# Attention and a gated FFN on one core: weight conversions moved some rounds later in the first stage, and the early FFN products dealt out anew

## The chip, the cores and the metric

One core of a Trainium2 chip runs the whole kernel in one launch. The metric is the device time of one execution in microseconds (us); the time before is the median of three runs, 660.65 us. TensorE is called PE here, VectorE DVE, ScalarE ACT, GpSimd POOL; SP is the queue that issues the DMAs.

## The reference

```python
# q, k, v: (4, 12, 448, 64), causal attention; its output as x: (1792, 768) float32
scores = where(mask, -1e9, q @ k.T / 8)
attn = exp(scores - max); attn = attn / (sum(attn) + 1e-9)
x = (attn @ v) reshaped to (B*S, H*D)
# FFN, d_ff = 1536
xn = x / sqrt(mean(x*x) + 1e-6) * rms_g
g = xn @ w_gate
out = ((g * sigmoid(g)) * (xn @ w_val)) @ w_out
```

## The kernel before, in words

The tokens are worked through in three groups. The first stage, some 50 us, is the attention of the first group, and everything in the change lies in it. It has 12 units p0 to p11 (a pair of heads, 256 queries). A unit goes through five steps: the scores on PE (L209), mask, maximum and subtraction on DVE (`softmax`, L225, four instructions), the exponentials with their sums on ACT (L228, four), the reciprocal sums `rs` on DVE (L239) and the scaling by them ("norms", L233, four instructions, on POOL save for p0 in part and p11, which is scaled on ACT, L231), then two sets of transposes on PE (L280: into bank `t` for the first head, into bank `x` for the second), their copies `pt` to SBUF (the first by ACT L286 or DVE L284, the second by DVE L284), and the products with v on PE (L309). Two units give one chunk c of x (0 to 5; p11 completes chunk 5). A chunk stands in PSUM, bank `a` or `y`, and `first_chunk` makes three things from it: `xh` (ACT, L396), the rounded value; `xl` (DVE, L397), its remainder; and `sq` (ACT, L346), its squares, which are added up in `acc` (POOL L107, for the last chunk DVE L348). `sq` has one buffer.

The column sums of `acc` (PE, L405) start the chain of the root mean square: a root on ACT (L414), reciprocal and diagonal on DVE (L417, L419), and a spreading product on PE (L423).

Beside the attention the first weight tiles s = 0, 1, 2, ... of the FFN are prepared. They come as 64-bit values (`load_w`, L456, three buffers) and are turned into float32 by `convert_ops`: `w_c` on ACT (L479), a shift on DVE (L480), a merge on DVE (L482), and a store (L484). `split_w` then makes the pair `w_h` (ACT, L492) and `w_l` (DVE, L494). A product "s1c4" is weight tile 1 with chunk 4 of x: three matmuls (L538, L539, L540) that need `w_h`, `w_l`, `xh` and `xl`. Fifteen of them (tiles 0 to 2, chunks 0 to 4) are laid into the first stage as early products, and the rest follow tile by tile.

The order is written out by hand. The stage is a list of steps, six to a round: in a round PE gets the scores of p+3, the products of p and the transposes of p+1. After each step a clock `now` ticks. `post(n, f)` puts f n ticks later, and the tables LOAD, CONVERT, SPLIT, SHIFT and MERGE give the tick of each weight tile's load and four preparing steps; READY_W and READY_X give the tick from which an early product may stand. Each engine works through its instructions in the order so made, and SP its DMAs; the times come from what they wait for. From tick 94 on the list ends and tile after tile is multiplied.

Of the kernel before, what the change touches and what calls it, by code (L numbers as in the profile page):

```python
# [14 lines left out]
ALU = mybir.AluOpType  # L15
# [8 lines left out]
NP = H // 2  # L24
# [13 lines left out]
for i in range(2 * 2 * NP, len(UNITS), NP):  # L38
    UNITS[i + 3: i + 6] = UNITS[i + 4: i + 6] + UNITS[i + 3: i + 4]
LAST = {(g, c): max(i for i, u in enumerate(UNITS) if u[0] == g and u[2] == c)  # L40
        for g in range(NG) for c in range(NP)}
# [3 lines left out]


T = dict(c0=0, c2=4, c3=4, c26=5, c36=5, c5=6, c56=7, exp=1, exp0=3, gt=1, hh=1, hl=4, ws=5, ld2=7,
         ld=4, ld1=11, lv=2, norm0=7, norm=6, norm1=2, r0=2, sq=1, acc=7, acc4=7, dg=0, spread=3, r1=5, so=3, wl=2, wl0=8, wl2=9, wl4=1, xl=2, xl0=9)
LOAD = (1, 15, 27, 37, 48, 60, 72, 84)
CONVERT = (16, 28, 38, 50, 64, 85, 88)  # L50
SPLIT = (34, 46, 58, 70)
SHIFT, MERGE = (24, 44, 54, 68, 78), (30, 46, 56, 70, 80)

READY_W, READY_X = (45, 57, 68), (40, 52, 64, 76, 87)
WR = 4
WARM = [6, 0, 0, 0]
EXTRA = 4
# [9 lines left out]
def attention_ffn(ctx: ExitStack, tc: tile.TileContext, qk0, qk1, qk2, v, v2, w, g, out, out2):  # L67
# [7 lines left out]
    nc = tc.nc  # L75
# [22 lines left out]
    def bank(tag, bufs=1):  # L98


        return ps.tile([P, W], F32, tag=tag, name=tag + "_ps", bufs=bufs)

    def f32(ap):
        return ap.bitcast(F32)

    def pool_op(out_, a, op, b):
        nc.gpsimd.tensor_tensor(out_, a, b, op=op)  # L107
# [28 lines left out]
    def post(delay, fn):  # L136
        if delay <= 0:
            fn()
        else:
            later.setdefault(now[0] + delay, []).append(fn)  # L140
# [7 lines left out]
    xr, xh, xl, acc, xq = {}, {}, {}, {}, {}  # L148
# [141 lines left out]
    def steps_a(p):  # L290


        if not 0 <= p < len(UNITS):
            return []
        g_, kind, c, k, _, base = UNITS[p]
        pr = hs[p]
        kb, nq = KB[kind], QUERIES[kind]

        def products():
            if g_ == 0 and base == 0:  # L300
                av[c] = bank("y").rearrange("p (s c) -> p s c", s=2) if c % 2 else av_ps
            at_ = av[c] if g_ == 0 else av_ps
            for h in range(1 + (kind == 2)):
                at = 0
                for j in range(NKB[kind]):
                    q0, n = ((0, 2 * P), (P, P))[j] if kind == 0 else (D * h, (P, D)[kind - 1])
                    a0 = at + (D * h if kind == 2 else 0)
                    for e in (0, 1):
                        nc.tensor.matmul(  # L309
                            at_[e * D: (e + 1) * D, p % 2, q0: q0 + n], raw_v[p][:kb, h, j, e, :],  # L310
                            pr["pt", e][:kb, a0: a0 + n], start=(j == 0), stop=(j == NKB[kind] - 1))
                    at += n if kind == 0 else P

        def copy():
            if p == ENDS[0] - 2:
                post(3, lambda: nc.scalar.activation(warm_up, eps, AF.Sqrt))
            if g_ == 0:
                if p == LAST[g_, c]:
                    x = av[c].rearrange("p s c -> p (s c)")
                    post(2, lambda: first_chunk(c, x))  # L320
                return
            if g_ == 2 and base == 0:
                if c < 3:
                    xq[c] = w64_p.tile([P, 2, XT], F32, tag="w64", name="xq")
                xr[g_, c] = xq[c % 3][:, c // 3]
            elif base == 0:
                xr[g_, c] = xr_p.tile([P, W], F32, tag="xr", name="xr")
            x = xr[g_, c][:, base: base + nq]
            if p == LAST[g_, c]:
                for j in range(1 + (g_ == 2)):  # L330
                    post(2 + j * (c < NP - 1), lambda j=j: square(g_, c, j))
            (nc.scalar.copy if g_ == 1 else nc.vector.tensor_copy)(x, av_ps[:, p % 2, :nq])

        return [products, copy]
# [4 lines left out]
    def first_chunk(c, x):  # L339

        last = c == NP - 1
        sq = rm_p.tile([P, W], F32, tag="sq", name="sq") if c else \
            rm_p.tile([P, W], F32, tag="acc", name="acc", bufs=2)

        def squares():
            nc.scalar.activation(sq, x, AF.Square)  # L346
            if last:
                nc.vector.tensor_tensor(acc[0, 0], acc[0, 0], sq, op=ALU.add)  # L348
                post(T["r0"], lambda: rms_first(column_sums(acc[0, 0])))
            elif c == 0:  # L350
                acc[0, 0] = sq
            else:
                post(T["acc"] if c < NP - 2 else T["acc4"], lambda: pool_op(acc[0, 0], acc[0, 0], ALU.add, sq))

        if last:
            squares()
        x_split(0, c, x)
        if not last:
            post(T["sq"], squares)

    sq2 = []

    def square(b, c, j):

        lo, hi = (HX * j, HX * (j + 1)) if b == 2 else (0, W)
        if c and j:
            if not sq2:
                sq2.append(rm_p.tile([P, W], F32, tag="rms", name="sq2", bufs=2))
            sq = sq2[0]
        else:  # L370
            sq = rm_p.tile([P, W], F32, tag="sq", name="sq") if c else \
                rm_p.tile([P, W], F32, tag="acc", name="acc", bufs=2)
        sq = sq[:, : hi - lo]
        nc.scalar.activation(sq, xr[b, c][:, lo: hi], AF.Square)  # L374
        if c == 0:
            acc[b, j] = sq
        else:
            post(3 if c < NP - 1 else 0, lambda: pool_op(acc[b, j], acc[b, j], ALU.add, sq))
        if b == 2:
            return  # L380
        if c == NP - 1:
            post(T["r1"], lambda: rms(b, [acc[b, 0]]))
        waiting.append((b, c))

    def split_x():
        if not waiting:
            return
        b, c = waiting.pop(0)
        x_split(b, c, xr[b, c])

    def x_split(b, c, x):

        gc = g_sb[:, c: c + 1]
        h = xx_p.tile([P, W], F32R, tag=f"xh{c}", name="xh")
        l = xx_p.tile([P, W], F32R, tag=f"xl{c}", name="xl")
        nc.scalar.mul(h, x, gc)  # L396
        post(T["xl0" if b == 0 and c < NP - 1 else "xl"], lambda: nc.vector.scalar_tensor_tensor(  # L397
            out=l, in0=x, scalar=gc, in1=f32(h), op0=ALU.mult, op1=ALU.subtract))
        xh[b, c], xl[b, c] = h, l

    def column_sums(sq):

        ps = bank("t")[:, : W // P]
        for i in range(W // P):
            nc.tensor.matmul(ps[:, i: i + 1], sq[:, P * i: P * (i + 1)], ones[:, :1],  # L405
                             start=True, stop=True)
        return ps
# [56 lines left out]
    def convert_ops(s):  # L464
# [6 lines left out]
        hf_ = raw_w.bitcast(F32)[:, :, 1]  # L471
        at2, at3, at5 = [T[n] for n in ("c26 c36 c56" if s < len(CONVERT) else "c2 c3 c5").split()]
        if s < len(MERGE):
            at2, at3, at5 = SHIFT[s] - CONVERT[s], MERGE[s] - CONVERT[s], MERGE[s] - CONVERT[s] + 8

# [11 lines left out]
    def split_w(s):  # L487
        if s < 2 * NU:
            t = wt[s]
            h = ws_p.tile([P, DM], F32R, tag="wh", name="w_h")  # L490
            l = ws_p.tile([P, DM], F32R, tag="wl", name="w_l")
            nc.scalar.copy(h, t)  # L492
            if s < NU + 2 * NF or s % 2:
                post(T[("wl0", "wl0", "wl2", "wl2", "wl4")[s] if s < 5 else "wl"], lambda: nc.vector.tensor_tensor(l, t, f32(h), op=ALU.subtract))  # L494
            else:
                post(T["wl"], lambda: pool_op(l, t, ALU.subtract, f32(h)))
            wt[s] = tuple(a.rearrange("p (k m) -> p k m", m=P) for a in (h, l))
            u = s - NU
            if 0 <= u < 2 * NF:
                pair[u % 2] = t  # L500
                if u % 2:
                    post(T["ws"], lambda v=u // 2, t0=pair[0], t1=t: quad_sums(v, t0, t1))
# [404 lines left out]
    with tc.manual_schedule():  # L907
# [25 lines left out]

        for fs, at_ in ((load_w, LOAD), (lambda n: convert(n), CONVERT), (split_w, SPLIT)):
            for n, t_ in enumerate(at_):
                at_tick(t_, lambda fs=fs, n=n: fs(n))
# [13 lines left out]
        def convert(s):  # L950
            for d, op in convert_ops(s):
                post(d, op)
# [12 lines left out]
        for s in range(2 * NU):  # L965
# [5 lines left out]
            if s % NU == 0:  # L971
                at, goal = done, ends[w_ + 1]
            if len(LOAD) <= s + 7 < NU:
                post(T["ld"], lambda s=s: load_w(s + 7))
# [6 lines left out]
            for k0 in (0, 2, 4):  # L981
# [7 lines left out]
                if w_ == 0 and i >= 73 and (i % 2 or i > 100):  # L989
                    split_x()  # L990
                if k0 == (0 if s < 3 else 4) and s + 3 >= len(SPLIT):
                    split_w(s + 3)
                if k0 == 4 and s + 5 >= len(CONVERT):
                    convert(s + 5)
# [127 lines left out]
```

## Time and profile before

| | |
|---|---|
| median of 3 runs | 660.65 us (660.17 to 661.35) |
| profiled execution | 660.94 us, of it 659.1 us in the span |
| PE busy | 650.7 us (99%) |
| DVE, ACT, POOL busy | 494.1 (75%), 388.7 (59%), 302.5 us (46%) |
| PE busy, 0 to 21.7 us | 19.94 us |
| PE busy, 21.7 to 30 us | 6.53 us of 8.30 |

Times below count from the start of the span. A matmul's listed time overlaps the next one's; what a sequence costs PE is the distance from start to start. On the other engines too a listed time ends some 0.1 us after the next instruction has started, so the distance of starts is the price there as well.

### The profile page before, as it was taken

How to read it: one execution, taken by the hardware profiler on the slowest of the kernel's cores; microseconds unless marked ns; L12 is line 12 of the kernel's file. 1: busy time of each engine (PE TensorE's matmuls, PEld its weight loads, DVE VectorE, ACT ScalarE, POOL GpSimd, SP SyncE). 2: the span in 40 equal slices, each digit the busy share in tenths (PEclk: the TensorE clock that was granted, in tenths of full speed). 3: DMA queues.
4: the chain of work that ended last, by engine and by line, in shares of the span. 5: the costliest groups of instructions: out<-in, count | busy, mean ns of one | idle time of the engine just before them, and what ended most of it. 6: DMA issues, size and time to landing. Idle time of an engine off the chain costs nothing.

```text
span 659.1 us, 12064 instructions
## 1 busy us (share of the span) xinstructions
PE 650.7 (99%) x4154; PEld 552.0 (84%) x4154; DVE 494.1 (75%) x1024; ACT 388.7 (59%) x852; POOL 302.5 (46%) x300
## 2 busy tenths in 40 slices
PE   9899999999999999999999999999999999999997
PEld 6567777777877787877787878888999999999997
DVE  6988997788886676767677663595776866889992
ACT  6996767766875567666666655435433434355540
POOL 4760403345543066886768788643424342402220
PEclk9999999999999999999999999999999999999999
DMA  8885997888896448585848655235666366473541
GB/s 284 287 257 204 293 282 237 291 292 236 260 322 222 137 146 277 188 297 191 255 156 252 206 183 196 88 118 184 240 218 230 123 225 218 152 221 96 156 144 61
DMA packets 71501, 138.82 MB, mean 211 GB/s; under 512 B 7760, under 2 KB 39376, under 8 KB 71440
## 3 DMA queue, kind: packets, MB, share of 16 engines
q1 hardware_dynamic: 71440, 138.05, 64.4%
q8 instruction: 33, 0.54, 0.3%
q14 instruction: 28, 0.23, 0.1%
HBM read 104.21 MB, written 33.82 MB: 209 GB/s over the span
## 4 chain that ended last, share of the span: by engine, by line
PE 90%; ACT 4%; DVE 2%; POOL 1%; issue 1%; DMA 1%; SPq 0%; DVEq 0%; POOLq 0%; ACTq 0%
PE m_ps L538 15%; PE m_ps L540 14%; PE m_ps L539 14%; PE s_ps L689 9%; PE m_ps L689 9%; PE a_ps L309 6%; PE t_ps L280 5%; PE y_ps L689 5%; PE x_ps L689 4%; PE s_ps L209 2%; ACT sp L228 2%; PE s_ps L217 1%; POOL sp L233 1%; PE x_ps L209 1%; PE x_ps L217 1%
## 5 line engine op out<-in xcount | busy, mean ns | idle before, releaser
L233 POOL TENSOR_SCALAR sp<-sp,rs 128x128 f32<-128x128 f32 (+3 forms) x162 | 126.2, 796 | 146.3 <-DVE rs L239 128.8
L538 PE MATMUL m_ps<-xh,w_h 128*128 128x512 f32 x276 | 117.1, 424 | 0.0
L540 PE MATMUL m_ps<-xh,w_l 128*128 128x512 f32 x276 | 108.3, 392 | 0.0
L539 PE MATMUL m_ps<-xl,w_h 128*128 128x512 f32 x276 | 108.2, 392 | 0.0
L228 ACT ACTIVATE sp<-sp,nm 128x128 f32<-128x128 f32 (+3 forms) x168 | 87.2, 522 | 12.1 <-DVE nm L225 12.1
L107 POOL TENSOR_TENSOR a_l<-w_q,a_h 128x768 fp32r<-128x768 f32 x24 | 47.9, 1996 | 79.6 <-ACT a_h L580 78.2
L286 ACT COPY pt<-t_ps 128x384 f32<-128x384 f32 (+1 forms) x69 | 34.3, 497 | 65.5 <-PE t_ps L280 65.2
L540 PEld LDWEIGHTS m_ps<-xh,w_l 128*128 128x128 f32 x276 | 51.9, 188 | 11.9
L538 PEld LDWEIGHTS m_ps<-xh,w_h 128*128 128x128 f32 x276 | 51.9, 188 | 11.4 <-issue 3.3
L539 PEld LDWEIGHTS m_ps<-xl,w_h 128*128 128x128 f32 x276 | 52.1, 189 | 8.0 <-issue 0.2
L538 PE MATMUL m_ps<-hh,w_h 128*128 128x512 f32 x144 | 58.1, 404 | 0.0
L280 PE MATMUL t_ps<-ident,sp 128*128 128x128 f32 (+1 forms) x348 | 56.9, 275 | 1.2 <-POOL sp L233 0.6
L280 PEld LDWEIGHTS t_ps<-ident,sp 128*128 128x128 f32 (+1 forms) x348 | 42.7, 137 | 18.3 <-POOL sp L233 4.2
L107 POOL TENSOR_TENSOR w_r<-w_r 128x384 f32<-128x384 f32 x48 | 51.6, 1085 | 12.2 <-DVE w_l L494 11.3
L540 PE MATMUL m_ps<-hh,w_l 128*128 128x512 f32 x144 | 56.2, 390 | 0.0
L539 PE MATMUL m_ps<-hl,w_h 128*128 128x512 f32 x144 | 56.2, 390 | 0.0
L225 DVE CUSTOM_DVE_ANT_0 sp<-s_ps,mask 128x128 f32<-128x128 f32 (+3 forms) x108 | 41.0, 428 | 19.7 <-PE s_ps L217 9.6
L309 PEld LDWEIGHTS a_ps<-pt,v_r 128*64 128x64 f32 (+1 forms) x816 | 36.5, 137 | 16.2 <-issue 6.9
L309 PE MATMUL a_ps<-pt,v_r 112*64 112x64 f32 (+2 forms) x816 | 46.1, 262 | 1.8 <-ACT sp L228 1.6
L580 ACT CAST a_h<-w_q 128x768 fp32r<-128x768 f32 (+1 forms) x48 | 35.0, 753 | 13.3 <-DMA w_q<-wz 5.6
L479 ACT ACTIVATE w_c<-w 128x768 f32<-128x768 f32 x36 | 33.0, 917 | 7.1 <-DMA w<-in_w 7.1
L107 POOL TENSOR_TENSOR acc<-acc,sq 128x384 f32<-128x384 f32 (+1 forms) x19 | 23.4, 1236 | 29.6 <-ACT sq L374 27.8
(212 smaller groups left out, 1661.1 us busy)
## 6 DMA issues: line engine op xcount, KB each, us to landing
w<-in_w SPq DMA_DIRECT2D x36, 768.0 KB, 5.2
w<-w_c SPq DMA_DIRECT2D x36, 384.0 KB, 5.7
w_r<-w SPq DMA_DIRECT2D x36, 384.0 KB, 5.0
qk_r<-in_qk SPq DMA_DIRECT2D x48, 256.0 KB, 5.1
qk_r<-in_qk SPq DMA_DIRECT2D x12, 512.0 KB, 4.1
v_r<-in_v SPq DMA_DIRECT2D x12, 448.0 KB, 4.8
v_r<-in_v SPq DMA_DIRECT2D x24, 192.0 KB, 4.2
wy<-w_r SPq DMA_DIRECT2D x24, 192.0 KB, 5.0
```

The costliest lines, as they stand in the source:

```text
L107: nc.gpsimd.tensor_tensor(out_, a, b, op=op)
L225: nc.vector.tensor_tensor_reduce(out=sp, in0=ps, in1=mk, scale=nsc, scalar=3.0e38, op0=ALU.add, op1=ALU.min, accum_out=nm)
L228: post(T["exp" if p >= ENDS[0] else "exp0"], lambda: nc.scalar.activation(sp, sp, AF.Exp, bias=nm, scale=-1.0, accum_out=sm))
L233: pr["norms"].append(lambda: (nc.gpsimd if p or not e else nc.vector).tensor_scalar(sp, sp, rs, 1.0, op0=ALU.mult, op1=ALU.mult))
L280: nc.tensor.transpose(ps[:kb, at: at + P], pr["sp"][e][:, o + kb * j: o + kb * (j + 1)], ident)
L286: nc.scalar.copy(pt[:kb, :at], ps[:kb, :at])
L309: nc.tensor.matmul(at_[e * D: (e + 1) * D, p % 2, q0: q0 + n], raw_v[p][:kb, h, j, e, :], pr["pt", e][:kb, a0: a0 + n], start=(j == 0), st ...
L538: nc.tensor.matmul(ps, wh[:, k, :], mh, start=(first and k == ks[0]), stop=False)
L539: nc.tensor.matmul(ps, wh[:, k, :], ml, start=False, stop=False)
L540: nc.tensor.matmul(ps, wl[:, k, :], mh, start=False, stop=(last and k == 5))
L580: nc.scalar.copy(h, src)
L689: nc.tensor.matmul(ps, a[x], b[y], start=first and n == 0, stop=last and n == 2, skip_group_check=True)
```

## The change

Three tables and some delays change; no instruction is added or taken away. Tile 1 is shifted and merged later (ticks 44 and 46 become 55 and 60); tiles 2, 3 and 4 are converted at 52, 64 and 88 in place of 38, 50 and 64; the splits of tiles 1, 2 and 3 stand at 61, 81 and 91 in place of 46, 58 and 70; the loads of tiles 4 to 7 move from 48, 60, 72, 84 to 61, 72, 87, 95. Chunks 1 to 3 of x are taken from PSUM six ticks later, with `xl` three ticks behind `xh` in place of nine and the squares six ticks behind in place of one. Tile 1 is ready for products from tick 69 (57 before), tile 2 from 87 (68).

```diff
-         ld=4, ld1=11, lv=2, norm0=7, norm=6, norm1=2, r0=2, sq=1, acc=7, acc4=7, dg=0, spread=3, r1=5, so=3, wl=2, wl0=8, wl2=9, wl4=1, xl=2, xl0=9)
-LOAD = (1, 15, 27, 37, 48, 60, 72, 84)
-CONVERT = (16, 28, 38, 50, 64, 85, 88)
-SPLIT = (34, 46, 58, 70)
-SHIFT, MERGE = (24, 44, 54, 68, 78), (30, 46, 56, 70, 80)
-READY_W, READY_X = (45, 57, 68), (40, 52, 64, 76, 87)
+         ld=4, ld1=11, lv=2, norm0=7, norm=6, norm1=2, r0=2, sq=1, sq4=6, acc=7, acc4=3, dg=0, spread=3, r1=5, so=3, wl=2, wl0=8, wl1=5, wl2=4, wl3=2, wl4=1, xl=2, xl0=9, xl1=3)
+LOAD = (1, 15, 27, 37, 61, 72, 87, 95)
+CONVERT = (16, 28, 52, 64, 88, 90, 97)
+SPLIT = (34, 61, 81, 91)
+SHIFT, MERGE = (24, 55, 70, 85, 92), (30, 60, 71, 86, 94)
+READY_W, READY_X = (45, 69, 87), (40, 52, 64, 76, 87)
...
-                    post(2, lambda: first_chunk(c, x))
+                    post(8 if 0 < c < NP - 2 else 2, lambda: first_chunk(c, x))
...
-            post(T["sq"], squares)
+            post(T["sq" if c < NP - 2 else "sq4"], squares)
```

DVE, where the reciprocals of p6 and the copy of p5's second transposes stand (`w_308` is the raw tile 1), before:

```order
L238 TENSOR_SCALAR sm<-sm 128x4
L239 RECIPROCAL rs<-sm 128x4
L480 TENSOR_SCALAR w_308<-w_308 128x768
L482 SCALAR_TENSOR_TENSOR w_c<-w_c,w_308 128x768
L284 COPY pt<-x_ps 128x384
L397 SCALAR_TENSOR_TENSOR xl<-y_ps,g_sb,xh 128x512
```

Now the shift and merge of tile 1 no longer stand ahead of that copy; they come some rounds further down. DVE, from the reciprocals of p11 to the chain of the root mean square, with the change (`w_494` is the raw tile 3, and the `w_l` is tile 2's):

```order
L238 TENSOR_SCALAR sm<-sm 128x4
L239 RECIPROCAL rs<-sm 128x4
L284 COPY pt<-x_ps 128x384 x2
L397 SCALAR_TENSOR_TENSOR xl<-a_ps,g_sb,xh 128x512
L480 TENSOR_SCALAR w_494<-w_494 128x768
L494 TENSOR_TENSOR w_l<-w_c,w_h 128x768
L482 SCALAR_TENSOR_TENSOR w_c<-w_c,w_494 128x768
L348 TENSOR_TENSOR acc<-acc,sq 128x512
L417 RECIPROCAL rc<-rc 128x4
L419 TENSOR_SCALAR dg<-ident,rc 128x128 x4
```

Before, L348 stood directly behind the last `xl` from bank `a`; now shift, `w_l` and merge stand between them. PE, from the products of p11 to the first product of tile 2, with the change (bank `m` takes s0 and s1, bank `s` takes s2):

```order
L309 MATMUL y_ps<-pt,v_r 64x256 x2
L309 MATMUL y_ps<-pt,v_r 64x128 x2
L538 MATMUL m_ps<-xh,w_h 128x512
L539 MATMUL m_ps<-xl,w_h 128x512
L540 MATMUL m_ps<-xh,w_l 128x512
L538 MATMUL m_ps<-xh,w_h 128x512
L539 MATMUL m_ps<-xl,w_h 128x512
L540 MATMUL m_ps<-xh,w_l 128x512
L405 MATMUL t_ps<-ones,acc 128x1 x4
L538 MATMUL s_ps<-xh,w_h 128x512
L539 MATMUL s_ps<-xl,w_h 128x512
L540 MATMUL s_ps<-xh,w_l 128x512
```

Ten early products now stand ahead of L405 and five behind it, all of tile 2; three of these stand between L405 and L423. Before, thirteen stood ahead of it and two (s1c4, s2c4) between L405 and L423.

## Rows read from the trace of the kernel before

**Rows 1.** Busy time by stretch: length, PE, PEld, DVE, ACT, POOL, clock, DMA

```profile
21.70:30.00 8.30, 6.53 (x52) 4.46 (x52) 7.38 (x28) 8.30 (x28) 6.52 (x11) 1.00 0.72 246
...
49.75:55.37 5.62, 5.55 (x26) 4.09 (x27) 4.16 (x10) 2.62 (x5) 0.00 (x0) 1.00 0.33 129
55.37:68.69 13.32, 13.32 (x63) 10.58 (x62) 12.94 (x27) 10.46 (x22) 2.06 (x2) 1.00 0.70 238
```

**Rows 2.** Timeline of PE, first stage: start, us, instruction [idle before it]

```profile
23.87 0.49 PE L280 MATMUL x_ps<-ident,sp 128*128 128x128 f32 x3
24.29 0.93 PE L209 MATMUL s_ps<-qk_r 64*128 64x128 f32 x8
26.83 0.87 PE L309 MATMUL a_ps<-pt,v_r 128*64 128x256 f32 x8 [1.61 <-ACT sp L228]
...
42.00 0.90 PE L280 MATMUL x_ps<-ident,sp 128*128 128x128 f32 x3
42.65 0.48 PE L538 MATMUL s_ps<-xh,w_h 128*128 128x512 f32 x1
```

**Rows 3.** Timeline of ACT around 22 us

```profile
21.70 0.93 ACT L479 ACTIVATE w_c<-w 128x768 f32<-128x768 f32 x1
22.54 0.39 ACT L228 ACTIVATE sp<-sp,nm 128x128 f32<-128x128 f32 x1
...
24.30 0.66 ACT L396 ACTIVATE xh<-y_ps,g_sb 128x512 fp32r<-128x512 f32 x1
```

**Rows 4.** Timeline of DVE around 25 us

```profile
24.42 0.17 DVE L238 TENSOR_SCALAR sm<-sm 128x4 f32<-128x4 f32 x1 [0.82 <-ACT sp L228]
...
24.73 0.53 DVE L480 TENSOR_SCALAR w<-w 128x768 int32<-128x768 int32 x1
25.29 1.01 DVE L482 SCALAR_TENSOR_TENSOR w_c<-w_c,w 128x768 int32<-128x768 int32 x1
26.22 0.54 DVE L284 COPY pt<-x_ps 128x384 f32<-128x384 f32 x1
26.69 0.73 DVE L397 SCALAR_TENSOR_TENSOR xl<-y_ps,g_sb,xh 128x512 fp32r<-128x512 f32 x1
```

**Rows 5.** Groups by line, 20 to 55 us: count, busy us, mean ns, idle before

```profile
L494 DVE TENSOR_TENSOR w_l<-w_c,w_h 128x768 fp32r<-128x768 f32 x4 | 3.9, 962 | 0.0
```

**Rows 6.** Timeline of POOL: norms of p6, squares of chunk 1, norms of p9

```profile
25.00 2.45 POOL L233 TENSOR_SCALAR sp<-sp,rs 128x128 f32<-128x128 f32 x4 [1.35 <-DVE rs L239]
27.42 1.29 POOL L107 TENSOR_TENSOR acc<-acc,sq 128x512 f32<-128x512 f32 x1
...
36.69 1.63 POOL L233 TENSOR_SCALAR sp<-sp,rs 128x128 f32<-128x128 f32 x4 [0.44 <-DVE rs L239]
```

**Rows 7.** Timeline of ACT and DVE at the end of the stage

```profile
46.10 1.28 ACT L316 ACT_TABLE_LOAD   x1
...
48.30 0.58 ACT L346 ACTIVATE sq<-y_ps 128x512 f32<-128x512 f32 x1
...
48.91 0.69 DVE L348 TENSOR_TENSOR acc<-acc,sq 128x512 f32<-128x512 f32 x1 [1.76 <-ACT sq L346]
```

**Rows 8.** Timeline of PE from the column sums on

```profile
49.75 1.02 PE L405 MATMUL t_ps<-ones,acc 128*128 128x1 f32 x8
...
52.34 1.10 PE L423 MATMUL t_ps<-dg,ones 128*128 128x512 f32 x2
52.88 0.79 PE L538 MATMUL m_ps<-xh,w_h 128*128 128x512 f32 x1
53.51 0.40 PE L539 MATMUL m_ps<-xl,w_h 128*128 128x512 f32 x1
```

**Rows 9.** Loads of v (L183), 19.9 to 47 us: from issue to landing

```profile
DMA to landing us min/median/max: 4.4/5.3/7.8
```

**Rows 10.** Timeline of DVE and PE behind the stage: bank m and its next user

```profile
65.67 0.68 DVE L555 TENSOR_TENSOR gr<-m_ps,rms 128x512 f32<-128x512 f32 x1
...
68.69 0.39 PE L538 MATMUL m_ps<-xh,w_h 128*128 128x512 f32 x1
```

More of the change, by code (lines that the diff above doesn't have):

```diff
@@ L396, in x_split @@
         nc.scalar.mul(h, x, gc)
-        post(T["xl0" if b == 0 and c < NP - 1 else "xl"], lambda: nc.vector.scalar_tensor_tensor(
+        post(T[("xl0", "xl1", "xl1", "xl1", "xl0", "xl")[c] if b == 0 else "xl"], lambda: nc.vector.scalar_tensor_tensor(
             out=l, in0=x, scalar=gc, in1=f32(h), op0=ALU.mult, op1=ALU.subtract))
@@ L493, in split_w @@
             if s < NU + 2 * NF or s % 2:
-                post(T[("wl0", "wl0", "wl2", "wl2", "wl4")[s] if s < 5 else "wl"], lambda: nc.vector.tensor_tensor(l, t, f32(h), op=ALU.subtract))
+                post(T[f"wl{s}" if s < 5 else "wl"], lambda: nc.vector.tensor_tensor(l, t, f32(h), op=ALU.subtract))
             else:
```

## Prediction, made before the changed kernel ran

> **What bounds the kernel now.** I read the stretches first. From 55.37 us on PE is busy in every stretch to its full length, and its clock is granted in full [rows 1]; behind the first stage a microsecond is gained only if PE comes out of that stage a microsecond earlier, and is lost if it must wait again later. In the first stage PE does wait: 6.53 of 8.30 us busy while ACT is busy for all 8.30 [rows 1]. So the question is when the first product of tile 3, the first work that stands in the same place in both orders, starts. Before it is 49.75 + 5.62 = 55.37 us: start of the column sums L405, and the stretch behind them [rows 1, 8].
>
> Then the timeline of PE for its gaps. The largest is ahead of the products of p5: the scores start at 24.29 and cost 0.85 (as long as the start-to-start distance of all such scores), so PE could go on at 25.14 and goes on at 26.83: 1.69 us [rows 2]. The others, from starts: 0.17 (p7), 0.53 (p9), about 0.5 (the transposes of p10, where 0.90 stands for what else is 0.49 [rows 2]), 0.2 ahead of L405, and behind it 0.23 ahead of L423 and 0.32 on `xl` of chunk 5, where L539 comes 0.63 after L538 in place of 0.31 [rows 8]. Together some 3.6 us; no order of the same work can win more here.
>
> **The change: what it takes away.** Nothing differs up to 21.70. There `w_c` of tile 2 stood on ACT; it costs 22.54 − 21.70 = 0.84, and the four exponentials of p6 behind it 24.30 − 22.54 = 1.76 [rows 3]. Without it they end at 23.46, so DVE, which waited 0.82 for them [rows 4], has the reciprocals of p6 0.84 earlier. Between these and the copy of p5's second transposes stood shift and merge of tile 1: 25.29 − 24.73 = 0.56 and 26.22 − 25.29 = 0.93 [rows 4]. Without both the copy waits for PE alone: its transposes start at 23.87 and land some 0.53 later [rows 2], and the copy runs from 24.40 to 24.86 (0.47 [rows 4]). The products of p5 then follow the scores at 25.14. The 1.69 us are gained whole, and nothing covers this place a second time.
>
> **What it moves there.** Shift and merge of tile 1, `w_l` of tile 1 and merge of tile 2 now stand further down, each where POOL scales a unit. That is the second term. Four norms take 1.63 us alone, and 2.45 where shift and merge lay beside them [rows 6]: about 0.8 us for one merge. An estimate step by step, each engine in its order with the costs above (PE: products 0.81, transposes 0.38 and 0.25 to 0.42, an early product 0.70; ACT: a copy 0.36, `xh` 0.57, `sq` 0.48; DVE: softmax 1.11, `xl` 0.66, all distances of starts in the same timelines):
>
> - Products of p6 at 28.3, of p7 at 31.0 (0.3 waiting for DVE). The reciprocals of p8 are done at 30.6; with merge 1 beside them its norms are half done at 32.4: PE waits 0.6.
> - Norms of p9 from 34.2, `w_l` of tile 1 beside them: whole at 36.6; PE waits 0.6 over both transposes.
> - POOL then has the squares of chunk 2 ahead of p10 (1.29 [rows 6]): norms of p10 start at 37.9 though their reciprocals are there at 36.9, merge 2 falls beside them, whole at 40.5. PE waits 1.0, and p10's second transposes stand at 40.5 where they stood at 42.0 to 42.4 [rows 2].
>
> In that part PE waits 2.5 us where it waited 1.2. Its next early product starts near 40.8 where it started at 42.65 [rows 2], but two early products fewer are done by then (1.40). What is left is a gain of some 0.45.
>
> The Trainium skill ("SBUF — State Buffer", section "Who interferes with whom") says that a DVE instruction with two SBUF inputs and a GpSimd instruction that reads SBUF exclude each other for the whole instruction. That speaks against this change, since it lays merges and `w_l` beside norms on which PE waits. The trace agrees in kind: 2.45 against 1.63 us [rows 6]. By the rule, merge and `w_l` cost their whole 0.93 to 0.96 us instead of 0.8, and the sum would be some 0.3 us higher.
>
> **The end of the stage.** By the steps above the transposes of p11 stand at 43.0, the second at 43.4, and PE is through s1c3, the products of p11, s0c4 and s1c4 at 43.6 + 0.77 + 0.81 + 1.40 = 46.6, or 46.9 with the short pauses between unlike work. L405 waits for `acc`. On ACT the copy of p11 ends at 43.9, `sq` of chunk 4 (0.48), `w_h` of tile 2 (0.73) and the table load (1.28, with its small instruction 1.4 [rows 7]) follow: `sq` of chunk 5 at 46.5 to 47.0. On DVE the copy ends at 44.4, and `xl` 0.66, shift of tile 3 0.57, `w_l` of tile 2 near 0.9 [rows 5], and merge of tile 3 0.9 stand ahead of L348: 47.4. From the start of L348 to L405 it took 49.75 − 48.91 = 0.84 [rows 7, 8], so L405 starts at 48.25, and PE stands for some 1.4 us ahead of it. Before, that wait was 0.2.
>
> Behind L405 three more early products stand (3 × 0.69 = 2.07), and they cover the chain: the waits of 0.23 and 0.32 go. 5.62 + 2.07 − 0.55 = 7.14, so tile 3 starts at 48.25 + 7.14 = 55.39 against 55.37. The sum is 0.0 us: the gap of 1.69 is closed, and comes back as waits for POOL and ahead of L405.
>
> **Behind the stage.** What was moved out is late work now: between the diagonal and the first `gr` DVE has `w_l` 3 and merge and shift 4, but not those of tile 6: 0.95 more, and shift and merge of tile 6 (1.5) come before the `gr` of tile 4; a tanh that now follows `w_c` of tile 6 on ACT may add 0.6. Bank m must be free for tile 6: its `gr` ends near 66.3, PE asks at 68.69 [rows 10], 2.4 us spare. DVE is 3.0 later counted from L405, PE 1.5: 0.9 us are left. I take 0; the cost begins when DVE falls 0.9 us further behind.
>
> On SP the load of v for p11 now stands behind the load of tile 5, which waits for merge 2 (39.1 by the above). Issued at 39.6, it lands after 4.4 to 7.8 us [rows 9]: 44.0 to 47.4, median 44.9, for products due at 44.5. Up to 45.7 this is hidden in the wait for L405.
>
> **Bounds.** If POOL isn't slowed at all, and `w_l` and merge hold nobody up, the last `sq` comes at 45.6 and L405 at 46.9 to 47.3: −1.3 to −0.9. With the longest landing of v, the products of p11 end at 48.2, L405 starts at 49.8: +1.6. I take the middle way, since the nearest row, the norms of p6, has just this neighbour.
>
> **The rivals.**
>
> *The relief arrives whole (faster).* PE waits for no norms and DVE is through merge 3 before the last `sq`. For it: ACT has 2.4 us less to do ahead of the last `sq` (`w_c` of tiles 4 and 5, `w_h` of tile 3), and ACT was the engine without a pause [rows 1]. Against it: 2.45 against 1.63 [rows 6], and the order of POOL. −1.3 to −2: 658.9 to 659.4. It decides from L405 at 46.9 or earlier.
>
> *Load of v late (slower).* One mechanism: SP waits for merge 2 with v of p11 behind it. Landing 7.5 us after issue makes L405 49.6: +1.4, 662.0 us. For it: 7.8 has been seen [rows 9]; against it: the median.
>
> *DVE is late behind the stage (slower).* Its backlog outgrows the 0.9 us ahead of tile 6, with 12.94 of 13.32 us busy there already [rows 1]. Two microseconds of further delay would cost 1.1 to 1.5 more: 661.8 to 662.2.
>
> **How the numbers follow.** The profiled execution took 660.94, 0.29 over the median, so a sum of 0.0 is 660.94 there and 660.65 as a median; I write 660.6. A measurement of this kernel can tell some 0.2%, 1.3 us, from no change. Forecast (−1.0 to +1.1, 659.6 to 661.7): 0.56. Relief whole: 0.23. Late v: 0.11. DVE backlog: 0.10. Hence faster 0.23, same 0.56, slower 0.21. The range leaves out the outer ends of both sides: 659.0 to 662.1.
>
> **What would show it.** Products of p5 near 25.1 with no idle time before them; norms of p8, p9 and p10 on POOL over 2.2 us each and PE waiting for them; PE idle 1 us or more ahead of L405, which starts at 47.5 to 49; no wait between L405 and tile 3; PE full from there. Wrong it would be if L405 starts under 47 (then faster), or if PE waits at tile 6 or for v of p11 (then slower).

## The result, and the profile after

The changed kernel took 665.08 us in the median of 6 executions (664.30 to 667.86), the kernel before 660.59 us in the same comparison: a ratio of 1.0071, 95% interval 1.0052 to 1.0091. It is 4.5 us slower. The forecast was 660.6 us and no change, with 662.1 as the upper end, so it was wrong. The profiled execution is the longest, 667.86 us with a span of 666.1; a second profile of the same kernel (below) is nearer to its median.

First the busy times by stretch, the columns as in [rows 1]; the cuts are L405 at 53.75 and the first product of tile 3 at 62.66.

```profile
21.70:30.00 8.30, 6.31 (x41) 4.24 (x39) 5.55 (x25) 7.28 (x30) 4.43 (x10) 0.84 0.67 237
30.00:45.00 15.00, 13.58 (x93) 8.47 (x91) 11.51 (x42) 11.04 (x34) 10.46 (x17) 0.97 0.50 157
45.00:53.75 8.75, 6.85 (x42) 4.53 (x41) 5.77 (x10) 7.60 (x14) 2.86 (x3) 1.00 0.59 180
53.75:62.66 8.91, 8.91 (x34) 7.00 (x35) 6.44 (x13) 3.79 (x6) 0.00 (x0) 0.81 0.73 220
62.66:76.00 13.34, 13.34 (x64) 10.59 (x63) 11.20 (x24) 9.86 (x21) 0.17 (x1) 1.00 0.72 234
```

ACT is no longer without a pause from 21.7 to 30 us (7.28 of 8.30), and DVE has less to do (5.55 where it was 7.38 [rows 1]). Both were meant to be relieved, and were. But PE is busy for less of that stretch than before, 6.31 us against 6.53, it stands again later, and the granted clock is under full in three stretches. Behind 62.66 PE is busy throughout, as before. From there to the end of the span it is 603.4 us, against 659.1 − 55.37 = 603.7 before: the loss lies ahead of tile 3, all of it.

The timeline of PE at the places of [rows 2] and [rows 8]:

```profile
24.57 0.93 PE L209 MATMUL s_ps<-qk_r 64*128 64x128 f32 x8
27.30 1.49 PE L309 MATMUL a_ps<-pt,v_r 128*64 128x256 f32 x8 [1.80 <-DMA v_r<-in_v]
...
50.04 0.87 PE L309 MATMUL y_ps<-pt,v_r 128*64 128x256 f32 x8 [0.53 <-DMA v_r<-in_v]
...
53.75 1.02 PE L405 MATMUL t_ps<-ones,acc 128*128 128x1 f32 x8 [1.25 <-DVE acc L348]
54.63 0.71 PE L538 MATMUL s_ps<-xh,w_h 128*128 128x512 f32 x1
55.15 0.63 PE L539 MATMUL s_ps<-xl,w_h 128*128 128x512 f32 x1
55.57 0.63 PE L540 MATMUL s_ps<-xh,w_l 128*128 128x512 f32 x1
...
58.36 1.02 PE L423 MATMUL t_ps<-dg,ones 128*128 128x512 f32 x2
```

The gap ahead of the products of p5 is still there, with another name in its bracket: v. L405 stands at 53.75 where it stood at 49.75. Behind it the matmuls follow each other at 0.42 to 0.43 us in place of 0.23: that is the lower of the clock's two levels, 1.2 GHz in place of 2.4.

What became of the relief is seen on ACT, and then on DVE, around 25 us [rows 3, 4]:

```profile
24.12 0.70 ACT L396 ACTIVATE xh<-y_ps,g_sb 128x512 fp32r<-128x512 f32 x1
24.70 0.41 ACT L228 ACTIVATE sp<-sp,nm 128x128 f32<-128x128 f32 x1
...
26.45 0.59 ACT L346 ACTIVATE sq<-y_ps 128x512 f32<-128x512 f32 x1
```

```profile
24.10 0.18 DVE L239 RECIPROCAL rs<-sm 128x4 f32<-128x4 f32 x1
24.68 0.56 DVE L284 COPY pt<-x_ps 128x384 f32<-128x384 f32 x1 [0.40 <-PE x_ps L280]
27.08 0.75 DVE L397 SCALAR_TENSOR_TENSOR xl<-y_ps,g_sb,xh 128x512 fp32r<-128x512 f32 x1 [1.84 <-ACT sq L346]
27.74 0.28 DVE L225 CUSTOM_DVE_ANT_0 sp<-s_ps,mask 128x128 f32<-128x128 f32 x1
...
29.05 0.18 DVE L239 RECIPROCAL rs<-sm 128x4 f32<-128x4 f32 x1
```

The copy `pt` of p5 is at 24.68 (26.22 before [rows 4]), as forecast. Then DVE stands for 1.84 us with `xl` at the head of its queue, and the bracket names the squares of chunk 1 on ACT. Behind `xl` on DVE stand the softmax of p8 and the reciprocals of p7, so POOL gets these at 29.05. Its norms of p7 start at 29.42, later than before: the head start of the reciprocals is spent on this one wait. These norms still end earlier, 31.04 against 31.87, since no shift and `w_l` lie beside them any more. POOL, norms of p7 before:

```profile
29.15 2.72 POOL L233 TENSOR_SCALAR sp<-sp,rs 128x128 f32<-128x128 f32 x4 [0.44 <-ACT w_c L479]
```

The same with the change, p7 to p10 [rows 6]:

```profile
29.42 1.62 POOL L233 TENSOR_SCALAR sp<-sp,rs 128x128 f32<-128x128 f32 x4 [3.33 <-DVE rs L239]
...
34.41 2.33 POOL L233 TENSOR_SCALAR sp<-sp,rs 128x128 f32<-128x128 f32 x4 [2.13 <-DVE rs L239]
39.15 2.32 POOL L233 TENSOR_SCALAR sp<-sp,rs 128x128 f32<-128x128 f32 x4 [2.41 <-DVE rs L239]
...
42.71 2.63 POOL L233 TENSOR_SCALAR sp<-sp,rs 128x128 f32<-128x128 f32 x4
```

The norms of p8, p9 and p10 take 2.32 to 2.63 us, each beside a merge or a `w_l`, as forecast (those of p10 beside a shift, too); alone four take 1.62.

One sentence ahead of the prediction is wrong: it says that the squares of chunks 1 to 3 go six ticks behind x. The delay of six holds for chunk 4 alone (the diff has it right); those of chunks 1 to 3 stay one tick behind `xh`. Since `xh` is now taken in the tick in which the four exponentials of the next unit are issued, one tick behind `xh` means behind these exponentials, 26.45 against 24.12 above. Before, the square followed `xh` directly.

### The profile page after: what moved, and what is told of

Its sections match the earlier page's. It is cut to its first block, busy times and chain, and to the rows that moved or that the text cites. A ratio compares the mean times of both kernels' runs of the same rounds, so it can differ in the third digit from the quotient of the medians.

```text
span 666.1 us, 12064 instructions
## 1 busy us (share of the span) xinstructions
PE 654.8 (98%) x4154; PEld 554.8 (83%) x4154; DVE 495.3 (74%) x1024; ACT 389.1 (58%) x852; POOL 301.9 (45%) x300
## 4 chain that ended last, share of the span: by engine, by line
PE 90%; DMA 3%; DVE 3%; ACT 2%; POOL 1%; issue 1%; SPq 0%; DVEq 0%; POOLq 0%; ACTq 0%
PE m_ps L538 14%; PE m_ps L539 14%; PE m_ps L540 14%; PE s_ps L689 10%; PE m_ps L689 9%; PE a_ps L309 6%; PE y_ps L689 5%; PE t_ps L280 5%; PE x_ps L689 4%; DMA v_r<-in_v 2%; PE s_ps L209 2%; PE s_ps L217 1%; POOL sp L233 1%; PE x_ps L209 1%; PE x_ps L217 1%
```

## The experiments

Each kernel was timed in 5 rounds against the kernel before on the same chip. The median of before was 661.37 beside the first four kernels, 660.78 beside the next four, 660.96 beside the next four and 660.97 beside the last three; across these groups ratios are compared, not times. "Tile 3" is the start of its first product, 55.37 before. Of the long table lines the diffs show only the part with the edit.

**1. The changed kernel once more.**

> The changed kernel once more, unaltered. Theory A (the order of work is at fault, and the half clock that PE was granted at 27 to 31 us and 55 to 58 us in the first trace is an extra that comes and goes): some 664.4 us, 3.8 above the kernel before, in executions with the clock granted in full, the first product of tile 3 near 59.2 us, and the waits ahead of the products of p5, for xl of chunk 2 and ahead of the column sums there as well. Theory B (the half clock is the loss): without it the time is within 1 us of the kernel before, 660 to 661.5.

Measured: 665.86 us, ratio 1.0072 (1.0061 to 1.0084). In this profile the clock is 1.00 in every stretch from 16 to 76 us, and still:

```profile
25.88 0.87 PE L309 MATMUL a_ps<-pt,v_r 128*64 128x256 f32 x8 [0.37 <-DMA v_r<-in_v]
...
27.88 0.50 PE L539 MATMUL m_ps<-xl,w_h 128*128 128x512 f32 x1 [0.42 <-DVE xl L397]
...
51.90 1.02 PE L405 MATMUL t_ps<-ones,acc 128*128 128x1 f32 x8 [1.35 <-DVE acc L348]
...
59.23 0.39 PE L538 MATMUL x_ps<-xh,w_h 128*128 128x512 f32 x1
```

Theory A: tile 3 is 3.9 us late with the clock at full, so the order is at fault first. The v of p5 came 1.4 us sooner here than in the first profile, and PE next waits for `xl`. DVE stood for 2.8 us ahead of three `xl`, all for squares.

**2. Squares behind xl** (the kernel as the sentence above wrongly had it):

```diff
-            post(T["sq" if c < NP - 2 else "sq4"], squares)
+            post(T["sq4" if c else "sq"], squares)
```

> In the changed kernel the squares of chunks 1 to 3 are written behind xl instead of ahead of it; ACT keeps nearly its order. Theory X (xl on DVE waits for the squares, which read the same bank and stand behind four exponentials on ACT; it held DVE 1.84, 1.22 and 0.40 us): these three waits go, the scores of p9 and what follows come 1 to 2 us earlier, 662.0 to 663.4 us. Theory V (the load of v for p5 and the end of the stage are the loss): less than 0.5 us is gained, 663.9 to 664.5.

Measured: 663.03 us, ratio 1.0030 (1.0019 to 1.0042), 2.8 us under the changed kernel beside it. That is within theory X. With `xl` ahead of the squares its wait is gone: that of chunk 1 starts at 24.94, where it started at 27.08. PE:

```profile
50.61 1.02 PE L405 MATMUL t_ps<-ones,acc 128*128 128x1 f32 x8 [1.18 <-DVE acc L348]
```

L405 is 1.3 us earlier than in the second profile above, still behind a wait. Not all of the 2.8 us is the wait of `xl`: the mean clock is 0.997 in three of eleven executions here, and was so in four of six of the changed kernel.

**3. v of p5 ahead of the load of tile 3 and the store of tile 0** (both two ticks later):

```diff
-LOAD = (1, 15, 27, 37,
+LOAD = (1, 15, 27, 39,
...
-            (at5, lambda: nc.sync.dma_start(out=w32[s], in_=t)),
+            (at5 + 2 * (s == 0), lambda: nc.sync.dma_start(out=w32[s], in_=t)),
```

> In the changed kernel the load of tile 3 and the store of tile 0 go two ticks later, behind the load of v for p5. Theory V (that load, issued behind both, lands 9.1 us later at 27.3 and holds the products of p5): they start near 25.2 instead of 27.3, with 1 to 2 us gained, 662.4 to 663.4. Theory X: DVE still stands until the squares of chunk 1 are done near 27, so the copies and softmax behind it are no earlier: under 0.6 us, 663.8 to 664.5.

Measured: 665.71 us, ratio 1.0072 (1.0060 to 1.0084): nothing is gained, as theory X says, though the time is above its range. The products of p5 start with no wait, and the first matmul that needs `xl` waits 0.87 us:

```profile
25.20 0.87 PE L309 MATMUL a_ps<-pt,v_r 128*64 128x256 f32 x8
...
27.65 0.50 PE L539 MATMUL m_ps<-xl,w_h 128*128 128x512 f32 x1 [0.87 <-DVE xl L397]
```

v was a second cover of the gap, `xl` the third.

**4. Without the later x** (weights and deal alone; `xl1` goes from 3 to 9, too):

```diff
-sq=1, sq4=6, acc=7, acc4=3
+sq=1, sq4=1, acc=7, acc4=7
...
-                    post(8 if 0 < c < NP - 2 else 2, lambda: first_chunk(c, x))
+                    post(2, lambda: first_chunk(c, x))
```

> The changed kernel with x taken from PSUM as before (two ticks behind its products, xl nine ticks behind xh), so only the weight conversions and the early products are changed. Theory X: the waits of DVE for the squares are gone, 661.5 to 663 us. Theory E (the end of the stage, with the column sums behind shift, w_l and merge on DVE and five early products behind them, is the main loss): still 663.5 to 664.5.

Measured: 661.78 us, ratio 1.0010 (1.0001 to 1.0018). Theory X: of the 0.72% that the changed kernel loses beside it, 0.62% come with the later x. PE still waits ahead of L405, for 0.58 us, and the clock is 0.999 or 1.000 in all twelve.

**5. The later x alone**, on the kernel before (with `xl1=3` and the change's line for `sq4`):

```diff
-sq=1, acc=7, acc4=7
+sq=1, sq4=6, acc=7, acc4=3
...
-                    post(2, lambda: first_chunk(c, x))
+                    post(8 if 0 < c < NP - 2 else 2, lambda: first_chunk(c, x))
```

> The kernel before with the later taking of x alone (copies of chunks 1 to 3 six ticks later with their subtraction xl three ticks behind, squares and sums of chunk 4 later), the weight tiles and the deal left as before. Theory A (this part alone holds the loss, since xl now waits for squares that stand behind four exponentials on ScalarE): 664 to 665.5, xl waits on ScalarE's squares for 2 us or more in sum, as in the changed kernel. Rival B (the loss needs both parts, since VectorE is late only with the subtractions w_l there as well): 661 to 662.5, and little waiting ahead of xl.

Measured: 663.36 us, ratio 1.0037 (1.0025 to 1.0049). The time is between the two theories: of the 4 us that the later x costs within the change, 2.6 come without the weights. The waiting is less than A said, one wait of 0.84 us, since here ACT's exponentials of p6 and DVE's shift and merge are still in the way of both. Behind it DVE has the reciprocals of p7 at 29.53 (28.77 before), and POOL starts the norms of p8 at 34.31 (32.85 before). That this one wait makes the loss is not shown: the 15th kernel is without it and no faster, though with another wait in its place.

**6. The deal alone:**

```diff
-READY_W, READY_X = (45, 57, 68), (40, 52, 64, 76, 87)
+READY_W, READY_X = (45, 69, 87), (40, 52, 64, 76, 87)
```

> The kernel before with nothing but the new deal of the early products (tiles 1 and 2 ready 12 and 19 rounds later in the table). Theory A: the deal costs little by itself, 661 to 662, as the kernel with conversions and deal but without the later x is at 661.8; TensorE then waits for the scores of the pairs that lost products. Rival B: the deal is what pushes the tail, 663 or more, and the later conversions win it back.

Measured: 663.66 us, ratio 1.0036 (1.0023 to 1.0049): B's size, by another way. In the profile L405 is at 49.77, as before, but tile 3 at 57.11, as more products are left behind L405 (7.34 us from one to the other, 5.62 before [rows 1]). Products that filled waits inside the stage stand behind L405 now, where there is none to fill. The profiled execution is the fastest, 662.39 us; three others took 663.7 to 663.9 at a full clock, and what these lose on top is not shown.

**7. Squares directly behind xh, as before the change:**

```diff
-            post(T["sq" if c < NP - 2 else "sq4"], squares)
+            post((T["sq"], 0, 0, 0, T["sq4"])[c], squares)
```

> The changed kernel with the squares of chunks 1 to 3 directly behind their copy xh on ScalarE (same tick), as they stood in the kernel before; all else as changed. Theory A (what costs is that xl stands behind squares that stand behind four exponentials): xl waits below 0.5 us in sum, 662.5 to 663.5, like the kernel with the squares written behind xl. Rival B (the square of 0.65 us then stands ahead of the exponentials, so scores and exps of each pair are late by that instead): 664 to 665.5.

Measured: 663.65 us, ratio 1.0040 (1.0025 to 1.0056); no `xl` of chunks 1 to 3 waits. That is near theory A and under B. DVE, then PE:

```profile
24.36 0.56 DVE L284 COPY pt<-x_ps 128x384 f32<-128x384 f32 x1 [0.41 <-PE x_ps L280]
25.00 0.75 DVE L397 SCALAR_TENSOR_TENSOR xl<-y_ps,g_sb,xh 128x512 fp32r<-128x512 f32 x1
...
26.97 0.18 DVE L239 RECIPROCAL rs<-sm 128x4 f32<-128x4 f32 x1
...
44.94 0.75 DVE L397 SCALAR_TENSOR_TENSOR xl<-a_ps,g_sb,xh 128x512 fp32r<-128x512 f32 x1
45.61 1.07 DVE L480 TENSOR_SCALAR w<-w 128x768 int32<-128x768 int32 x1
46.60 0.95 DVE L494 TENSOR_TENSOR w_l<-w_c,w_h 128x768 fp32r<-128x768 f32 x1
...
48.34 0.68 DVE L348 TENSOR_TENSOR acc<-acc,sq 128x512 f32<-128x512 f32 x1
```

```profile
25.11 0.87 PE L309 MATMUL a_ps<-pt,v_r 128*64 128x256 f32 x8
...
28.27 0.87 PE L309 MATMUL y_ps<-pt,v_r 128*64 128x256 f32 x8
...
40.33 0.89 PE L280 MATMUL x_ps<-ident,sp 128*128 128x128 f32 x3
...
49.16 1.02 PE L405 MATMUL t_ps<-ones,acc 128*128 128x1 f32 x8 [1.34 <-DVE acc L348]
...
56.52 0.39 PE L538 MATMUL x_ps<-xh,w_h 128*128 128x512 f32 x1
```

The reciprocals of p7 come 2.08 us sooner than in the changed kernel, and tile 3 2.7 us sooner than in its second profile. Yet its executions spread from 661.82 to 665.57, with a mean clock of 0.995 to 0.997 in four of six.

**8. The column sums behind two products of tile 2:**

```diff
-norm1=2, r0=2, sq=1, sq4=6
+norm1=2, r0=4, sq=1, sq4=6
```

> The changed kernel with the column sums of L405 two ticks later, so that TensorE does products of tile 2 in the time in which it waited for the sum of squares (1.25 to 1.35 us ahead of L405). Theory A (that wait is a part of the loss, since nothing behind it waits for L405 itself until the diagonal): 664.2 to 664.9, no wait of over 0.3 ahead of L405. Rival B (the chain from L405 to the first tile that needs the root, with its copy on ScalarE, is as long as the products left behind it, and the wait comes back ahead of the spread or of tile 3): 665.5 to 666.

Measured: 662.91 us (662.70 to 663.33), ratio 1.0029 (1.0018 to 1.0040); a clock of 0.999 or 1.000 in all six. The gain is twice what A gave it: 1.35 us is the wait, seen in tile 3 (57.68 against 59.23), and the rest is the clock, which no longer falls in any execution.

```profile
51.67 1.02 PE L405 MATMUL t_ps<-ones,acc 128*128 128x1 f32 x8
...
57.68 0.39 PE L538 MATMUL x_ps<-xh,w_h 128*128 128x512 f32 x1
```

**9. The kernel before with its column sums first** (r0=0 there), to make that wait where nothing else is changed:

```diff
-norm1=2, r0=2, sq=1
+norm1=2, r0=0, sq=1
```

> The kernel before with the column sums of L405 two ticks earlier, ahead of two products of tile 2 instead of behind them, so that TensorE stands for about 1.5 us ahead of L405, as it does in the changed kernel; nothing else is moved. Theory A (after such a wait the granted clock falls to half in most executions, and this is a part of what the changed kernel loses): clock 0.995 to 0.998 in most executions, 663 to 664.5, with a wide spread. Theory B (the clock is no part of it; the two products are only done later): clock 0.999 or 1.000 in all, 662.0 to 662.6.

Measured: 661.78 us, ratio 1.0020 (1.0009 to 1.0030).

```profile
49.80 1.02 PE L405 MATMUL t_ps<-ones,acc 128*128 128x1 f32 x8 [1.56 <-DVE acc L348]
...
56.45 0.39 PE L538 MATMUL x_ps<-xh,w_h 128*128 128x512 f32 x1
```

Neither theory alone: nine executions at 1.000 lie between 661.57 and 662.17, at the lower end of B's range and under it, and three at 0.997, 0.997 and 0.995 took 663.52, 663.38 and 665.09. The clock can fall after this wait, which costs 1.7 to 3.4 us over the nine, but here it does so in a quarter of the executions.

**10. Both repairs**, the edits of the seventh and the eighth kernel together:

> The changed kernel with both repairs: squares of chunks 1 to 3 directly behind xh, and the column sums behind two products of tile 2. Theory A (the two waits are the whole loss): the first product of tile 3 at 55.2, that is 56.52 of the kernel with the squares alone less its 1.34 of waiting; clock 0.999 or 1.000; 660.3 to 661.0, level with the kernel before. Rival B (the new deal and the later loads cost something of their own, as in the kernel with the deal alone): 662 to 663.

Measured: 660.53 us, ratio 0.9997 (0.9989 to 1.0006), the clock 0.999 or 1.000 in all eleven. Theory A: with the two waits out, the changed kernel is level with the kernel before.

```profile
25.80 0.87 PE L309 MATMUL a_ps<-pt,v_r 128*64 128x256 f32 x8 [0.64 <-DMA v_r<-in_v]
...
45.56 0.87 PE L309 MATMUL y_ps<-pt,v_r 128*64 128x256 f32 x8 [0.42 <-DMA v_r<-in_v]
...
49.38 1.02 PE L405 MATMUL t_ps<-ones,acc 128*128 128x1 f32 x8
...
55.35 0.39 PE L538 MATMUL x_ps<-xh,w_h 128*128 128x512 f32 x1
```

**11. Both repairs and v ahead of the weight tiles** (the store of tile 0 as in the third kernel):

```diff
-LOAD = (1, 15, 27, 37, 61, 72, 87, 95)
+LOAD = (1, 15, 27, 39, 61, 76, 87, 95)
```

> As the one with both repairs, and each v load of p5, p7 and p11 issued ahead of the load of a weight tile, not behind it. Theory A (waits of TensorE for v_r of 0.4 at p11, and in some executions at p5, go): 0.3 to 0.8 below the kernel with both repairs, first product of tile 3 at 54.5 to 55.0, 659.8 to 660.6. Rival B (the weight tiles then land later and their splits wait, or POOL's norms hold the pairs up anyway): no gain, or 0.5 to 1 us more.

Measured: 660.76 us, ratio 0.9999 (0.9990 to 1.0008). The waits for v are gone in the profile, and 0.37 us came back ahead of L405; tile 3 at 54.99. No gain that can be measured, as in rival B.

**12. Without the later x, column sums behind two products** (the edits of the fourth and the eighth):

> The changed kernel without the later taking of x (661.8), with the column sums behind two products of tile 2. Theory A (its wait of 0.58 ahead of L405 is the only part that the sums' place can give back): 661.0 to 661.5, clock 1.000. Rival B (the products there wait for the splits of tile 2, or the spread comes late): 661.8 or more.

Measured: 660.55 us, ratio 0.9993 (0.9984 to 1.0001): under theory A's range, the lowest ratio here, and not to be told from no change or from the kernel with both repairs.

**13. The same, with the load of tile 5 behind v of p11** (in LOAD 76 for 72):

> The changed kernel without the later taking of x and with the column sums two ticks later (660.55), and the load of tile 5 behind the v load of p11. Theory A (the one wait left in that kernel, 1.14 for v_r ahead of the products of p11, is due to the load of a tile ahead of v in SyncE's queue): that wait below 0.5, 659.6 to 660.2, faster than the kernel before. Rival B (v of p11 is issued late for another reason, such as the release of its buffer): no change, 660.3 to 660.8.

Measured: 661.03 us, ratio 1.0005 (0.9996 to 1.0014). The wait for v at p11 is gone, but v of p5 came 0.49 us late in this profile, and the median did not fall: the cause is theory A's, the gain is not.

**14. The changed kernel with that one edit**, the load of tile 5:

```diff
-LOAD = (1, 15, 27, 37, 61, 72, 87, 95)
+LOAD = (1, 15, 27, 37, 61, 76, 87, 95)
```

> The changed kernel with nothing but the load of tile 5 behind the v load of p11. Open is what makes the clock fall in most executions of the changed kernel but in 3 of 12 of the kernel before with the same wait ahead of L405. Theory A (two waits close together, for v_r at p11 and for the sum at L405): without the first, clock under 0.999 in a third of the executions or fewer, 664.0 to 664.8. Rival B (the wait ahead of L405 alone, and chance): clock 0.997 in more than half as before, 665 to 666.

Measured: 666.11 us, ratio 1.0075 (1.0062 to 1.0088), clock 0.997 in four of five. Rival B: what p11 no longer waits for v it waits ahead of L405, whose time DVE sets.

```profile
51.76 1.02 PE L405 MATMUL t_ps<-ones,acc 128*128 128x1 f32 x8 [1.85 <-DVE acc L348]
```

**15. The later x alone, repaired** (the fifth kernel with the edits of the seventh, the eighth and the third):

> The kernel before with the later taking of x alone, repaired: squares directly behind xh, column sums two ticks later, v of p5 ahead of the load of tile 3. Open is whether the later x, whose aim shows as the gap of 1.6 ahead of the products of p5, gives anything once its waits are gone. Theory A (the gap goes and nothing takes its place): products of p5 at 25.2, tile 3 at 54.0 to 54.6, 659.3 to 660.0. Rival B (the weight tiles' subtractions on VectorE then delay the pairs in its place): 660.5 to 662.

Measured: 664.63 us, ratio 1.0061 (1.0047 to 1.0075), worse than both theories.

```profile
26.95 0.86 PE L309 MATMUL a_ps<-pt,v_r 128*64 128x256 f32 x6 [1.04 <-DVE pt L284]
...
54.58 1.10 PE L423 MATMUL t_ps<-dg,ones 128*128 128x512 f32 x2 [1.57 <-DVE dg L419]
```

With the old tables DVE's shift and merge hold the copy of p5, so the gap only changes its name a fourth time; that is near rival B. And with the old deal two products fewer are left between L405 and L423: r0=4 spends them ahead of L405, and PE stands for the diagonal instead, again with a clock of 0.997 in four of five.

## Why the prediction was wrong, point by point

*"The 1.69 us are gained whole, and nothing covers this place a second time."* This step failed, twice over. The relief of ACT and DVE came as forecast: the copy of p5 at 24.68, the products possible near 25.1. But the v of p5 was issued at 17.6 and took 9.1 us before the change, so it landed at 26.7, only 0.1 us ahead of the end of the gap; the range of landings that the prediction used [rows 9] begins with the loads behind it. And on DVE `xl` now stood for the squares. The second is the one that costs: with v in time (third kernel) nothing was won, with the squares moved (seventh) the products of p5 stand at 25.11 with no wait, and L405 came 2.7 us earlier than in the second profile of the changed kernel. By ratios of the medians the squares are worth 0.32%, 2.1 us.

Behind this lies a dependency that the prediction left out. `xl` and `sq` both only read chunk c in its PSUM bank; the built program still lets the second in program order wait for the first, as the brackets show in the profile. Before, `sq` stood ahead of `xl` too, but right behind `xh`, which `xl` needs anyway, and the wait was short enough not to show: no `xl` of before has a bracket. The change put four exponentials, 1.75 us, between `xh` and `sq` (24.70 to 26.45). The wrong sentence ahead of the prediction hides this: with squares six ticks behind `xh` and `xl` three, `xl` would come first and not wait, as in the second kernel. The Trainium skill states this dependency: "PSUM — Partial Sum Buffer", section "PSUM bank collisions raise a hardware error", has the compiler's scheduler order any two instructions of different engines that touch one bank in the same 32 partitions, two readers too. The trace agrees: `xl` stood 1.84 us for squares that only read its bank. Letting both read at once was not tried.

*The norms of p8, p9 and p10 lengthened; PE waits 2.5 us instead of 1.2; a gain of some 0.45 is left.* The mechanism held, 2.32 to 2.63 us each, which is 0.7 to 1.0 over the 1.62 alone where 0.8 was forecast. The steps, too: in the kernel with the squares at `xh`, products of p6 stand at 28.27 (28.3 forecast), of p7 at 30.74 (31.0), the second transposes of p10 at 40.33 (40.5). They were right for a kernel whose `xl` does not wait.

*L405 at 48.25 with PE idle for 1.4 us ahead of it.* The wait held, 1.25 to 1.35 us, with shift, `w_l` and merge ahead of L348. Its place did not: 51.90 to 53.75, by the delays above. Where these are gone (seventh kernel) it is 49.16, still 0.9 late, and DVE sets it. The last `xl` from bank `a` starts there at 44.94, not 44.4, and the shift of tile 3 takes 0.99 us from start to start, not 0.57; the squares of chunk 4 on POOL lie beside it, but that these slow it is not shown. What failed most here is the price. The wait was costed as its own length; in three of the first six and four of the second six executions the mean clock was 0.995 to 0.997, and in the first profile the products behind the wait ran at half speed. The four executions with a clock of 1.000 took 664.3 to 664.7 us, the seven with 0.995 to 0.997 took 665.7 to 667.9. With the sums two ticks later the kernel gained 2.8 us by the ratios, of which the wait is 1.35 and the clock the rest.

*From L405 to tile 3 7.14 us, no wait in it.* 7.33 us where the clock stayed up; right to 0.2 us. *Behind the stage 0.* Right: 603.4 to 604.9 us from tile 3 to the end in all profiles, with or without the change. The rival of a late DVE behind the stage did not come.

*v of p11.* Hidden, it was said, up to a landing at 45.7. PE waited 0.43 to 0.53 for it, and the 14th kernel shows that it was hidden in effect: without it the wait ahead of L405 is longer by as much.

*The sum of 0.0.* The kernel that was priced is the seventh, in which `xl` does not wait for the squares but PE still waits ahead of L405. Its tile 3 is at 56.52, not 55.39: the terms that were in the sum come out 1.1 us short, 0.9 of it ahead of L405. The kernel with both repairs does measure 0.0, 660.53 us against 660.96, tile 3 at 55.35 against 55.37. But its column sums are moved, which gives back the very wait that the sum had paid for, so it does not confirm the balance; that the two agree is luck. The two terms that were missing are the wait of `xl` for `sq`, 2.1 us by the ratios, and the clock behind the wait ahead of L405, some 1.5 (2.8 less the wait of 1.35). With the 1.1 these make 4.7 of the 4.5 to 4.8 us measured. The slower side had 0.21, on rivals that did not come.

What stays open is why the clock falls in 19 of 28 executions of the changed kernel and its near kin (first, third, seventh and 14th with the first comparison) after a wait of 1.25 to 1.85 us, but in 3 of 12 of the kernel before after 1.56 us.

## What to carry to other kernels

When a table moves the reader of a PSUM bank on one engine, look up every other engine's reader of that bank: whichever comes second in program order waits, and what is put ahead of the first one is put ahead of the second too. A gap that is to be closed has as many covers as things arrive near its end; list them all with their times (here the copy, v and `xl`) before it is called gained. Where PE must stand for a microsecond or more just ahead of dense work, put ready products there if enough are left behind them: in the eighth kernel this gained 2.8 us, in the 15th, with two products fewer behind L405, the wait came back ahead of the diagonal's product.

## What the runs showed of the hardware that was not expected

The granted clock. In the kernels in which PE stood for some 1.2 us or more just ahead of L405 or L423 (the changed kernel in both comparisons, and the second, third, seventh, ninth, 14th and 15th kernel), the mean clock was 0.997 or less in 29 of 56 executions. In the others, where no wait there is over 0.6 us, it was so in none of 72, nor in any of the 84 of the kernel before, although that one stands for 1.61 us ahead of the products of p5 [rows 2]. The changed kernel's first profile stands there for 1.80 us, and falls to half (the 1.49 us of the products at 27.30, where they take 0.87). So the length of the wait alone does not say in which execution the clock falls, and no run here shows what does.

In the last 75 us the same matmuls took 339 ns in the profiles of four kernels (the changed one's second, the second, the seventh and the 15th) and 336 in others, the kernel before among them, though nothing in that stage differs; these four have 604.5 to 604.9 us from tile 3 to the end, where most have 603.4 to 604.0 (the tenth has 604.4, with 336). From 584 us on, in the kernel with the squares at `xh`, and in the one with the sums later:

```profile
L689 PE MATMUL s_ps<-a_h,oh 128*128 128x384 f32 x54 | 18.3, 339 | 0.0
```

```profile
L689 PE MATMUL s_ps<-a_h,oh 128*128 128x384 f32 x54 | 18.1, 336 | 0.0
```

This is why the start of tile 3, and not the span, was compared above.
